# A decode step with cached attention: the pair loop rolled into seven rounds, batch by batch

## The chip, the cores and the metric

The kernel runs on one core of a Trainium2 chip. The time is device microseconds of one execution, the median over runs. The core has a matrix engine (PE, whose weight loads the profile lists apart as PEld), a vector engine (DVE), a scalar engine (ACT), a general engine (POOL) and SP, which here only issues loads. Sixteen DMA engines move the data from memory (HBM) into the on-chip store; each load that SP issues is spread over all of them.

## The reference

Eight batches, one new token each (x is 8 x 1 x 512). All arithmetic is in float32.

```python
xn = _layernorm(x)
# attention over a cache of 8192 positions, 8 KV heads of 128, 4 query heads on each
q = (xn @ wq).reshape(8, 1, 32, 128)
p = softmax(einsum("bhqd,bhkd->bhqk", q, repeat(k_cache, 4)) * 128 ** -0.5)
a = einsum("bhqk,bhkd->bhqd", p, repeat(v_cache, 4)).reshape(8, 1, 4096) @ wo
# token mixer on the same xn, hidden size 1792, inputs normalised once more
u = gelu(layernorm(xn)[..., None] * w1 + b1)      # (8, 512, 1792)
y = u @ w2 + b2
out = x + a + y
```

k_cache and v_cache are 8 x 8 x 8192 x 128 each, 268 MB apiece. Everything else is small beside them: wq and wo are 8.4 MB each.

## The kernel before, in words

**Pairs.** Two neighbouring KV heads of one batch form a pair: 8 MB of K and 8 MB of V. There are 32 pairs and one step for each (`duo_step`, L390). The order is by head group: pair i has group i // 8 and batch i % 8 (L105).

**Slots and loads.** The on-chip ring has five slots of 4 MB. K of a pair takes two slots, 1 and 2 or 0 and 1 in turn (`home`, L88); V takes slots 3 and 4. All loads of the caches are issued by SP in one queue, in an order written out by hand (`plan`, L93 to L101, taken by `load_next`, L103). A step n runs so:

1. First half of the scores (`score_half`, L381): for each quarter of the head dimension DVE transposes K in place in blocks of 32 (`turn_duo`, L255), and PE multiplies it with the query kept in `Z` (`qk_duo`, L261). After this half one slot is free, and SP issues the load of K for step n + 1.
2. Second half of the scores.
3. The row maximum (`top_duo`, L278), first half of the values of step n - 1 (`pv_duo`, L302: PE, with V as the moving operand), the exponential of step n on ACT (`exp_duo`, L283), second half of the values of step n - 1. Then slots 3 and 4 are free, and SP issues the load of V for step n.
4. `send_duo` (L296) lays the exponentials out for the next step's values: two PE matmuls, two DVE transposes.
5. At the end of a group of eight, `q_place_duo` (L242) fills `Z` for the next eight pairs. `place_duo` (L318) normalises and folds four finished pairs at a time into `OT`, which the output projection reads at the end. `take_duo` (L312) copies the finished values out of PE's accumulators.
6. `mix` (L365) does 5, 5 or 4 pieces of the token mixer: a gelu on ACT, and a scale and an addition on POOL (`mx_step`, L350). Fourteen pieces make a batch; `mx_begin` and `mx_end` are around them.

All engines run programs in the order written; the kernel is one straight line of instructions. PE's program is the longest: most matmuls in float32 are two passes, each with its weight load.

**Head and tail.** Before step 0 wq is loaded into slots 2 and 3, q is projected (`q_project`, L222), and 16 small matmuls on constants (`SHIFT`, L218 to L220) stand ahead of it. In the last step wo is loaded into free slots behind the last V, and the output projection follows as its pieces land.

The one function with all of this, with the line numbers of the profile:

## Time and profile before

| | |
|---|---|
| median of 3 runs | 1291.61 us (1291.28 to 1291.95) |
| profiled execution, its own time | 1291.54 us |
| its span, first to last instruction | 1289.5 us |
| granted clock of PE, mean | 0.803 |
| moved by DMA | 554.39 MB, 430 GB/s over the span |
| recorded instructions | 10806 |

The page gives, for each engine, busy time, share of the span and count of instructions; then the span in 40 slices; then the DMA queues. Queue q1 is SP's. Rows marked "instruction" are DMA packets that bring program code to the engines. In rows of instruction groups, the numbers after the first bar are busy time in us and the mean of one in ns, and after the second bar the engine's idle time before them with what ended it. "Landing" is the moment at which all of a load has arrived.

### The profile page before, as it was taken

The page shows a single profiled execution, that of the slowest core. Times are in us where ns is not written, and L with a number is a line of the kernel's source. Part 1 is how long each engine was busy: PE and PEld are TensorE (multiplying, and loading weights), DVE is VectorE, ACT ScalarE, POOL GpSimd, SP SyncE. Part 2 cuts the span into 40 slices and gives each one's busy share as a digit, 9 for nine tenths or more (in the row PEclk, how much of TensorE's full clock was granted, in tenths as well). Part 3 has the DMA queues.
Part 4 walks back from the last instruction along what each step waited for, and adds up shares of the span by engine and source line. Part 5 has one row for each costly group of instructions (what it writes and reads, how often), then busy time and mean ns, then how long its engine had stood idle before and what let it go on. Part 6 is the DMA issues. An engine that isn't in the chain of part 4 may idle for free.

```text
span 1289.5 us, 10806 instructions
## 1 busy us (share of the span) xinstructions
PE 755.4 (59%) x4662; PEld 161.9 (13%) x4662; DVE 677.8 (53%) x509; ACT 207.0 (16%) x311; POOL 226.5 (18%) x241
## 2 busy tenths in 40 slices
PE   4377455665456666565565656575454774466676
PEld 1111011111011111011110111111011110011112
DVE  3656654455644465654465644466644565544461
ACT  0002222121222121222111221212222000000000
POOL 0003323121332122233113322212332000000000
PEclk9667877997778896687886887877778878768879
DMA  9999999999999999999999999999999999999997
GB/s 407 433 431 448 427 427 438 434 431 438 431 431 440 431 427 444 425 432 442 427 434 438 431 434 434 436 436 427 436 434 431 432 436 435 429 440 432 427 428 323
DMA packets 11011, 554.39 MB, mean 430 GB/s; under 512 B 1324, under 2 KB 1356, under 8 KB 1748
## 3 DMA queue, kind: packets, MB, share of 16 engines
q1 hardware_dynamic: 10836, 553.67, 99.3%
q8 instruction: 36, 0.59, 0.2%
q14 instruction: 11, 0.09, 0.0%
q0 software_dynamic: 96, 0.02, 0.0%
q10 hardware_dynamic: 32, 0.02, 0.0%
HBM read 553.69 MB, written 0.02 MB: 429 GB/s over the span
## 4 chain that ended last, share of the span: by engine, by line
DMA 73%; DVE 22%; PE 4%; issue 0%; SPq 0%; DVEq 0%
DMA raw<-in_A_k_cache_dram 69%; DVE raw L257 22%; PE acc L267 3%; DMA raw<-in_A_wo_dram 2%; DMA raw<-in_A_wq_dram 2%; PE misc L227 0%; PE acc L308 0%; PE hb L444 0%; SPq L125 0%; DVEq L257 0%; SPq L82 0%; PE misc L285 0%; DVE macc L451 0%; DVEq L451 0%
## 5 line engine op out<-in xcount | busy, mean ns | idle before, releaser
L257 DVE STREAM_TRANSPOSE raw<-raw 128x2048 f32<-128x2048 f32 x256 | 565.4, 2275 | 242.0 <-DMA raw<-in_A_k_cache_dram 242.0
L267 PE MATMUL acc<-raw,z 128*32 128x512 f32 x2048 | 372.6, 812 | 481.4 <-DVE raw L257 480.1
L308 PE MATMUL acc<-raw,pt 128*32 128x512 f32 x2048 | 246.9, 624 | 12.0 <-DMA raw<-in_A_v_cache_dram 11.8
L354 POOL TENSOR_SCALAR g<-g,pad 128x512 f32<-128x512 f32 x112 | 77.8, 694 | 577.7 <-ACT g L353 577.7
L267 PEld LDWEIGHTS acc<-raw,z 128*32 128x32 f32 x2048 | 47.4, 124 | 789.9 <-DVE raw L257 491.2
L355 POOL TENSOR_TENSOR macc<-macc,g 128x512 f32<-128x512 f32 x112 | 142.0, 1268 | 9.3
L293 ACT ACTIVATE t2k<-acc,nb 128x512 f32<-128x512 f32 x32 | 22.0, 687 | 649.8 <-DVE nb L287 649.8
L300 DVE STREAM_TRANSPOSE pt<-misc 128x512 f32<-128x512 f32 x64 | 45.9, 717 | 141.3 <-PE misc L299 136.9
L353 ACT ACTIVATE g<-hb,pad 128x512 f32<-128x512 f32 x112 | 87.1, 777 | 192.8 <-POOL macc L355 191.5
L308 PEld LDWEIGHTS acc<-raw,pt 128*32 128x32 f32 x2048 | 66.2, 115 | 178.1 <-issue 150.0
L287 DVE CUSTOM_DVE_ANT_0 t2k<-misc,hmask 128x128 f32<-128x128 f32 x32 | 9.3, 291 | 122.5 <-PE misc L285 122.5
L299 PE MATMUL misc<-t2k,send 128*128 128x512 f32 x128 | 65.3, 633 | 2.7 <-ACT t2k L293 2.7
L280 DVE TENSOR_REDUCE mr<-acc 128x1 f32<-128x512 f32 x32 | 22.1, 690 | 50.8 <-PE acc L267 50.8
L316 ACT COPY ob<-acc 128x512 f32<-128x512 f32 x32 | 18.8, 586 | 118.9 <-PE misc L332 55.1
L347 POOL MEMSET macc<- 128x512 f32 x8 | 4.2, 527 | 182.0 <-PE misc L359 152.0
L353 ACT ACT_TABLE_LOAD x24 | 30.8, 1283 | 17.9 <-PE hb L345 17.6
L422 ACT ACT_TABLE_LOAD x24 | 30.8, 1283 | 0.4
L332 PE MATMUL misc<-ob,pick 128*32 128x512 f32 (+2 forms) x72 | 29.0, 545 | 0.7 <-ACT ob L316 0.7
L299 PEld LDWEIGHTS misc<-t2k,send 128*128 128x128 f32 x128 | 22.2, 193 | 44.7 <-issue 41.9
L334 DVE TENSOR_TENSOR t2k<-misc,keep 32x512 f32<-32x512 f32 (+2 forms) x9 | 5.7, 629 | 22.6 <-PE misc L332 22.6
L227 PE MATMUL misc<-raw,ob 128*32 128x512 f32 x64 | 10.4, 806 | 10.9 <-DMA raw<-in_A_wq_dram 10.9
L438 PE MATMUL acc<-raw,ot 128*32 128x512 f32 x56 | 8.0, 717 | 4.6 <-DMA raw<-in_A_wo_dram 4.6
(76 smaller groups left out, 122.4 us busy)
## 6 DMA issues: line engine op xcount, KB each, us to landing
raw<-in_A_v_cache_dram SPq DMA_DIRECT2D x4, 4096.0 KB, 35.5
raw<-in_A_wq_dram SPq DMA_DIRECT2D x2, 4096.0 KB, 17.2
raw<-in_A_k_cache_dram SPq DMA_DIRECT2D x2, 4096.0 KB, 31.9
raw<-in_A_wo_dram SPq DMA_DIRECT2D x1, 4096.0 KB, 28.6
raw<-in_A_wo_dram SPq DMA_DIRECT2D x1, 2048.0 KB
raw<-in_A_wo_dram SPq DMA_DIRECT2D x1, 1024.0 KB, 31.3
raw<-in_A_wo_dram SPq DMA_DIRECT2D x1, 512.0 KB
raw<-in_A_wo_dram SPq DMA_DIRECT2D x2, 256.0 KB, 32.3
```

The lines of the kernel that those rows point to most:

```text
L257: nc.vector.transpose(t, t)
L267: nc.tensor.matmul(SD[i][c * W:(c + 1) * W, :].rearrange("p (t j) -> p t j", j=W), Z[:, q, b, (1 - k) * REP:(1 - k) * REP + W], t[:, c * C ...
L280: nc.vector.tensor_reduce(mr, SD[i], AX.X, ALU.max)
L293: nc.scalar.activation(p, SD.pop(i), AF.Exp, bias=nb, scale=SCALE, accum_out=LD[e][:, o:o + 1])
L299: nc.tensor.matmul(m, send[:, k, :], p, start=True, stop=True)
L300: nc.vector.transpose(PT[k][:, :CH_T * W], m)
L308: nc.tensor.matmul(OD[i][j * W:(j + 1) * W, :].rearrange("p (c d) -> p c d", c=NCH), PT[k][:, t * W:(t + 1) * W], v[:, t], start=(not k an ...
L332: nc.tensor.matmul(mv, pick[:, c, :], ob[:, :n, c * DH:(c + 1) * DH], start=(c == 0), stop=(c == NCH - 1))
L353: nc.scalar.activation(g, hb, AF.Gelu_apprx_tanh, bias=b1t[:, j:j + 1], scale=w1t[:, j:j + 1])
L354: nc.gpsimd.tensor_scalar(g, g, w2t[:, j:j + 1], 1.0, op0=ALU.mult, op1=ALU.mult)
L355: nc.gpsimd.tensor_add(acc, acc, g)
L422: nc.scalar.activation(small.tile([P, 1], F32, name="warm"), nil, AF.Exp)
```

## The change

Pairs are taken batch by batch: pair i is batch i // 4 and head group i % 4, so that four steps in a row belong to one batch, and successive loads are successive 8 MB of the caches. Steps 0 and 1 and steps 30 and 31 stay written out. Steps 2 to 29 become a loop of seven rounds with four steps each. Inside it, the addresses of the loads, of the query taken for a batch, of the mixer's batch and of the output column come from registers. The loop is asked to synchronise its rounds by registers (`iteration_sync="reg_based"`).

- The query for all 32 pairs is put into `QZ` at the start, and `q_set` copies four pairs at a time into the smaller `Z`.
- The results of four pairs are normalised (`total`) and placed (`place_at`) together, once per batch, for one column of `OT`.
- The mixer does one batch per round, in pieces of 5, 5, 4 and 0; batch 7 is done ahead of the loop, seven pieces in each of the steps 0 and 1. The first piece writes `acc`, so that no clearing is needed; the scale is now a `tensor_tensor` with a broadcast operand.
- The bound of the exponential takes three DVE instructions in place of `tensor_tensor_reduce`.
- V of a round's fourth step, which the first step of the next round reads, is loaded on a semaphore `landed`. PE waits for it ahead of the values and takes the count back; before the loop PE raises it once for the first round. The other waits that the framework would make for this load are declared away (`apart`, `let_go`).
- The 16 matmuls on constants are gone.

```diff
+NG = HKV // 2
+FIRST = 2
+ROUNDS = B - 1
...
-MIX = (5, 5, 4)
+MIX = (5, 5, 4, 0)
...
-SHIFT = 16
...
+    pairs = {id(c): c.rearrange("b (g h) s d -> (b g) (h s d)", h=2) for c in (kc, vc)}
+    landed = tc.alloc_semaphore("landed")
+    def load(c, i, at, part=None, own=False):
+        flat = pairs[id(c)]
+        if isinstance(i, int):
+            rows = flat[i].rearrange("(p m) -> p m", p=P)
         else:
-            nc.sync.dma_start(t[:, x], rows[:, x])
+            rows = flat[bass.ds(i, 1)].rearrange("a (p m) -> p (a m)", p=P)
...
+        d = nc.sync.dma_start(slot(at, n).rearrange("p s m -> p (s m)"), rows)
+        if own:
+            d.then_inc(landed, 16)
+            tc.no_tile_sem_insts.add(d.ins.name)
+            tc.add_to_no_dep_group("landed", d.ins)
+        return d
...
-    idle = misc()
-    for j in range(SHIFT):
-        nc.tensor.matmul(idle[j % NB * W:(j % NB + 1) * W, :W], ident[:, :W], rep[:, 0, :W], start=True, stop=True)
...
+    def q_set(i, g, n):
+        dst = Z[:, :, :, REP:].rearrange("p g q (a k r) -> p g q a k r", k=2, r=REP)
         for a in range(NB):
             x = slice(a * W, (a + 1) * W)
-            nc.scalar.copy(dst[x, :, :, a, 0, :], src[x].rearrange("p (q b) r -> p q b r", b=B))
+            src = QZ[x, i:i + n] if isinstance(i, int) else QZ[x, bass.ds(i, n)]
+            nc.scalar.copy(dst[x, g:g + n, :, a, 0, :], src)
...
-        nc.vector.tensor_tensor_reduce(big()[:, :P], m[:, :P], hmask, -SCALE, 3.0e38, ALU.add, ALU.min, nb)
+        nc.vector.tensor_tensor(t, m[:, :P], hmask, op=ALU.add)
+        nc.vector.tensor_reduce(nb, t, AX.X, ALU.max)
+        nc.vector.tensor_scalar(ns, nb, -SCALE, None, op0=ALU.mult)
...
+    def total(lo, hi):
+        x = slice(lo * W, hi * W)
+        m = misc()
+        for g in range(lo, hi):
+            nc.tensor.matmul(m[g * W:(g + 1) * W, :1], ohg, lr[:, g:g + 1], start=True, stop=True)
+        nc.vector.reciprocal(rl[x], m[x, :1])
+    def place_at(lo, hi, col):
+        x = slice(lo * W, hi * W)
+        m = misc()
         for c in range(NCH):
+            for g in range(lo, hi):
+                nc.tensor.matmul(m[g * W:(g + 1) * W, :DH], pick[:, c, :], OB[:, g, c * DH:(c + 1) * DH],
+                                 start=(c == 0), stop=(c == NCH - 1))
...
     def mx_step(j):
         nc.scalar.activation(g, hb, AF.Gelu_apprx_tanh, bias=b1t[:, j:j + 1], scale=w1t[:, j:j + 1])
-        nc.gpsimd.tensor_scalar(g, g, w2t[:, j:j + 1], 1.0, op0=ALU.mult, op1=ALU.mult)
-        nc.gpsimd.tensor_add(acc, acc, g)
+        nc.gpsimd.tensor_tensor(g if j else acc, g, w2t[:, j:j + 1].to_broadcast([P, D]), op=ALU.mult)
+        if j:
+            nc.gpsimd.tensor_add(acc, acc, g)
...
+    def softmax_and_values(n, then, ready=None):
+        mr = top(n)
+        if ready is not None:
+            nc.tensor.wait_ge(landed, 16)
+            nc.tensor.sem_inc(landed, -16)
+        if n:
+            values(n - 1, 0, ready is not None)
+        p = exps(n, mr)
+        if n:
+            values(n - 1, 1, ready is not None)
+        d = then()
+        if ready is not None:
+            apart(d)
+        send_on(p)
...
-    for i in range(N_PR):
-        duo_step(i)
+    score_half(1, False)
+    softmax_and_values(1, lambda: load(vc, 1, 3))
+    nc.tensor.sem_inc(landed, 16)
+    take(0)
+    for j in range(NF // 2, NF):
+        mx_step(j)
+    warm()
+
+    with tc.For_i(FIRST, FIRST + ROUNDS * NG, NG, iteration_sync=SYNC) as i:
+        col = i - FIRST
+        j = 0
+        for n in range(FIRST, FIRST + NG):
+            score_half(n, True)
+            load(kc, i + (n + 1 - FIRST), home(n + 1))
+            score_half(n, False)
+            softmax_and_values(n, lambda: load(vc, i + (n - FIRST), 3, own=(n == FIRST + NG - 1)),
+                               n == FIRST or None)
+            take(n - 1)
+            if n == NG - 1:
+                total(0, NG)
+                q_set(i + (NG - FIRST), 0, NG)
+            if n == NG:
+                place_at(0, NG, col)
+            if n == FIRST:
+                mx_end(col * 2)
+                mx_begin(col)
+            for _ in range(MIX[n - FIRST]):
+                mx_step(j)
+                j += 1
+            warm()
```

## The prediction

> **What bounds the kernel now.** I read the page's busy lines and its DMA table first, then the chain of waits, then the last microseconds in windows, and then the timeline around one step boundary.

> The page:

> ```profile
> span 1289.5 us, 10806 instructions
> PE 755.4 (59%) x4662; PEld 161.9 (13%) x4662; DVE 677.8 (53%) x509; ACT 207.0 (16%) x311; POOL 226.5 (18%) x241
> GB/s 407 433 431 448 427 427 438 434 431 438 431 431 440 431 427 444 425 432 442 427 434 438 431 434 434 436 436 427 436 434 431 432 436 435 429 440 432 427 428 323
> q1 hardware_dynamic: 10836, 553.67, 99.3%
> q8 instruction: 36, 0.59, 0.2%
> q14 instruction: 11, 0.09, 0.0%
> ```

> No engine is over 59% busy, while the load queue q1 keeps all 16 DMA engines at 99.3% from the first slice to the last but one. So DMA sets the time, and a change in an engine's work counts only if a load is issued too late, or if DMA time itself changes. Two rows beside q1 are not data: 36 packets of 0.59 MB and 11 of 0.09 MB that fetch instructions. 0.59 MB is 63 bytes for each of PE's 4662 + 4662 instructions, so q8 is PE's code, one packet of 16.4 KB per 259 instructions, one about every 1289.5 / 36 = 35.8 us. q14 carries the other engines' code in packets of 8.2 KB.

> Does 0.2% of traffic matter? A load has landed only when the slowest of its DMA engines is done. The chain of waits (start us, length us, what) shows K loads from issue to landing:

> ```profile
> 266.22 28.58 DMA raw<-in_A_k_cache_dram
> ...
> 304.96 29.47 DMA raw<-in_A_k_cache_dram
> ...
> 615.46 29.69 DMA raw<-in_A_k_cache_dram
> ...
> 655.32 28.44 DMA raw<-in_A_k_cache_dram
> ...
> 887.29 29.53 DMA raw<-in_A_k_cache_dram
> ```

> Three of the five (those issued at 304.96, 615.46 and 887.29) take 0.9 to 1.2 us longer than the other two, 1.0 on the mean. They stand 310.5 and 271.8 us apart, which is 8.7 and 7.6 of PE's fetch intervals. I read that as PE's fetches going around eight DMA engines, with every eighth hitting the one that is already last. The windows over the end of the loads test it (columns: window, length, busy us of PE, PEld, DVE, ACT, POOL with counts, clock, DMA share, GB/s):

> ```profile
> 1278.00:1279.00 1.00, 1.00 (x8) 0.23 (x4) 0.00 (x0) 0.00 (x0) 0.00 (x0) 0.50 0.81 334
> 1279.00:1280.00 1.00, 1.00 (x12) 0.27 (x8) 0.00 (x0) 0.00 (x0) 0.00 (x0) 0.87 0.65 272
> 1280.00:1281.00 1.00, 1.00 (x12) 0.26 (x8) 0.00 (x0) 0.00 (x0) 0.00 (x0) 1.00 0.59 250
> 1281.00:1282.00 1.00, 1.00 (x16) 0.34 (x12) 0.00 (x0) 0.00 (x0) 0.00 (x0) 1.00 0.55 227
> 1282.00:1283.00 1.00, 0.97 (x12) 0.06 (x4) 0.00 (x0) 0.00 (x0) 0.00 (x0) 1.00 0.51 207
> 1283.00:1284.00 1.00, 0.76 (x8) 0.16 (x8) 0.00 (x0) 0.00 (x0) 0.00 (x0) 1.00 0.50 199
> 1284.00:1285.00 1.00, 0.84 (x20) 0.38 (x16) 0.00 (x0) 0.59 (x1) 0.00 (x0) 1.00 0.28 107
> 1285.00:1286.00 1.00, 0.96 (x28) 0.53 (x24) 0.00 (x0) 0.00 (x0) 0.00 (x0) 1.00 0.05 18
> ```

> A load's 128 equal rows give each of 16 engines the same share, yet the engines do not finish together: a fifth is done soon after 1278, half by 1283, and the last after 1285. The late half have run some 7 us behind the early ones. That spread is what the instruction packets have cost, as far as I can see: 36 / 8 = 4.5, so up to five hits on one engine, 7 / 5 = 1.4 us each. The other two readings of the price of a hit are 1.0 (the three long loads) and, from q8's share (0.15 to 0.25% of 16 x 1289.5 us over 36 packets), 0.86 to 1.43. I take 1.3, nearest to the end spread because that is the whole delay, and keep 0.86 and 1.43 as bounds.

> **The boundary between two steps.** This timeline (start, length, engine, line, idle before and its releaser) shows the cover that loop overhead would have:

> ```profile
> 633.16 1.98 PE L299 MATMUL misc<-t2k,send 128*128 128x512 f32 x4
> 633.29 0.33 SPq L111 DMA_DIRECT2D raw<-in_A_v_cache_dram  x1
> 634.32 1.57 DVE L300 STREAM_TRANSPOSE pt<-misc 128x512 f32<-128x512 f32 x2 [4.33 <-PE misc L299]
> 645.25 17.66 DVE L257 STREAM_TRANSPOSE raw<-raw 128x2048 f32<-128x2048 f32 x8 [9.35 <-DMA raw<-in_A_k_cache_dram]
> 647.82 3.72 PE L267 MATMUL acc<-raw,z 128*32 128x512 f32 x16 [12.08 <-DVE raw L257]
> 655.32 0.33 SPq L111 DMA_DIRECT2D raw<-in_A_k_cache_dram  x1
> 664.58 3.64 PE L308 MATMUL acc<-raw,pt 128*32 128x512 f32 x32 [0.56 <-DMA raw<-in_A_v_cache_dram]
> ```

> A K load is issued at 655.32 while the V load ahead of it lands near 664.5, when PE's wait for it ends, so the queue is about 9.2 us deep at that point. At the boundary DVE idles 9.35 us, PE 12.08, and SP issues nothing from 633.6 to 655.3. A late start of DVE costs DMA time only beyond 9.35 + 9.2 = 18.5 us.

> **The change part by part.** (1) *Code.* The unrolled steps 2 to 29 become one body run seven times. What PE executes per step, with the rows of ACT and POOL that part 5 needs:

> ```profile
> L267 PE MATMUL acc<-raw,z 128*32 128x512 f32 x2048 | 372.6, 812 | 481.4 <-DVE raw L257 480.1
> L308 PE MATMUL acc<-raw,pt 128*32 128x512 f32 x2048 | 246.9, 624 | 12.0 <-DMA raw<-in_A_v_cache_dram 11.8
> L299 PE MATMUL misc<-t2k,send 128*128 128x512 f32 x128 | 65.3, 633 | 2.7 <-ACT t2k L293 2.7
> L293 ACT ACTIVATE t2k<-acc,nb 128x512 f32<-128x512 f32 x32 | 22.0, 687 | 649.8 <-DVE nb L287 649.8
> L353 ACT ACTIVATE g<-hb,pad 128x512 f32<-128x512 f32 x112 | 87.1, 777 | 192.8 <-POOL macc L355 191.5
> L354 POOL TENSOR_SCALAR g<-g,pad 128x512 f32<-128x512 f32 x112 | 77.8, 694 | 577.7 <-ACT g L353 577.7
> L355 POOL TENSOR_TENSOR macc<-macc,g 128x512 f32<-128x512 f32 x112 | 142.0, 1268 | 9.3
> ```

> (2048 + 2048 + 128) / 32 + 1 = 133 matmuls, 266 instructions with weight loads, 1064 in four steps. The new per-batch work (placing four pairs, 16 calls of two passes; four sums; mixer begin and end) adds 88: about 1152, or 4.4 packets a round. If the body stays loaded from round to round, six of seven rounds fetch nothing: 36 - 6 x 4.4 = 9.6 packets are left, two at most on any of the eight engines instead of five. Three hits fewer at 1.3 us: **-3.9 us**, bounds 3 x 0.86 = -2.6 and 3 x 1.43 = -4.3. If it is fetched anew in each round, nothing is gained (rival 1). No row here shows a backward branch, so both stand; I take the first because the eight-way rotation of 16.4 KB packets looks like eight places of 256 instructions, and the body needs six at most.

> (2) *The loop itself*: branches, register additions, waits on registers, the first and last entry. No row shows them. From below: nothing, under the idle stretches above. From above: 18.5 us per round would have to be passed before any of it shows, so a few microseconds for refilling an engine's code are hidden too. What isn't hidden is setup before the first load (SP's first issue is on the path) and after the last. I take +0.2, 0 to 0.5. If the cover were gone, each us would cost 7.

> (3) *V on its own semaphore.* V of a round's fourth step is awaited by PE just ahead of the values matmuls, where the row at 664.58 waits for V already. Behind that wait stand those matmuls and, on SP, the next V load, as before. Cost 0; upper bound is rival 2.

> (4) *Order of pairs.* Each load is still 8 MB contiguous in 128 rows of 64 KB; only which one follows changes. 0, though a gain or loss inside HBM is not excluded: the load rate of 430 to 440 GB/s is flat over all head groups, so I allow 0.5 us either way.

> (5) *Mixer.* The multiplication becomes POOL TENSOR_TENSOR, 1268 instead of 694 ns by L355. A mix step is ACT's 777 ns and these two in turn, 0.78 + 0.69 + 1.27 = 2.74 us, and grows to 3.3, with the gaps between them some 3.5. Five steps take 2.9 us more, and ACT idles 649.8 / 32 = 20.3 us before each exponential: hidden. The first two steps now carry seven each, and there it is close:

> ```profile
> 75.49 3.78 PE L299 MATMUL misc<-t2k,send 128*128 128x512 f32 x4 [2.66 <-ACT t2k L293]
> 94.03 0.69 ACT L293 ACTIVATE t2k<-acc,nb 128x512 f32<-128x512 f32 x1 [18.50 <-DVE nb L287]
> 101.28 11.08 DVE L257 STREAM_TRANSPOSE raw<-raw 128x2048 f32<-128x2048 f32 x5 [1.44 <-DMA raw<-in_A_k_cache_dram]
> ```

> Step 0's send ends at 79.3 and the mixer's first matmuls a microsecond later; seven steps begun near 80.5 end near 102 to 105, so step 1's exponential comes about 10 us later than 94.03. PE's send and DVE's two small transposes stand behind it, and DVE would turn K(2) from about 108 instead of 101.28. That spends 6.6 of the 9.2 us of queue, once: +0.2, 0 to 1.

> (6) *Softmax bound.* One DVE instruction pair becomes three instructions. ACT's 20.3 us of idle time ahead of the exponential are spent waiting for DVE's result, so this one comes later by what the extra two cost. Bounds: nothing, and two short DVE instructions of the size of the 0.7 us transpose half above, 1.4 us; I take 0.5. Behind it stand the send and the small transposes, whose end at 635.9 has DVE's 9.35 us of idle time after it: hidden, as are the register-addressed copies of q on ACT, which has no mixer work in the fourth step. The dropped 16 idle matmuls only shorten the head.

> **Sum.** From the profiled execution's own 1291.54 (span 1289.5 and 2.0 around it; the median 1291.61 is the same to 0.1): -3.9 + 0.2 + 0.2 = -3.5, so **1288.0**. Its own range is 1286 to 1290.

> **Rivals.**
> 1. *The code is fetched again in every round* (the slower side). Place: q8 and q14. A round then fetches the five or six blocks it touches and perhaps one beyond: 42 to 49 packets in the loop and some 6 outside. Spread evenly that is 6 or 7 per DMA engine, +1.3 to +2.6 us; if a block always comes through the same engine, 8 or 9, +3.9 to +5.2. The small engines add to it: DVE's 64 compute instructions a round (by the code) with waits and registers span two packets of half the size, 14 to 21 in all, and through one engine at 0.65 us that is 9 to 14 us, up to 7 over today's spread. It decides from the sixth hit on one engine. Time 1293 to 1299, middle 1295. For: nothing in the trace shows code being kept. Against: the rotation over eight. [...]
> 2. *Something still waits for V at the round's edge.* PE would start its scores with V at 664.6 instead of 647.8, the four quarters take 4 us, and the K load goes out near 669, 4.5 us after the queue ran dry: with some 1.9 us to restart (what the first slice lost: 407 of 433 GB/s over 32.2 us) 6.4 us a round, 1288.0 + 45 = 1333; at the first entry alone, 1294.4. Against: the change gives V its own semaphore.
> 3. *Fetches don't set the pace* (the late finish of half the engines has another cause). Then the sum is +0.4: 1292. Against: the spacing of the long loads.

> **Chances.** Forecast 0.56, rival 1 0.25, rival 2 0.08, rival 3 0.11. About 0.2% (2.6 us) is what a measurement tells from no change: below 1289.0 is faster, above 1294.2 slower. Faster: most of the forecast's share, 0.50. Slower: two thirds of rival 1 and most of rival 2, 0.24. Within: 0.26. For 8 in 10 the range runs from 1285.5 (one hit left per engine) to 1297 (most of rival 1).

> **What would show it.** q8 near 10 packets with q14 below 11; no K load longer than its neighbours by 1 us; DMA share falling to nothing within some 3 us at the end instead of 7. Rival 1: q8 at 45 or more and a spread over 7 us. Rival 2: a hole in DMA's share once a round. I am wrong if q8 falls to 10 and the time stays.

## The result, and the profile after

The changed kernel takes 1300.57 us (1299.37 to 1301.66) against 1291.57: a ratio of 1.0068, 95% interval 1.0055 to 1.0081, so 9 us slower. The forecast was 1288.0, with a range from 1285.5 to 1297; the measured time lies above it, on the other side of the kernel before.

The page after, the rows that answer to those of before:

```profile
span 1298.1 us, 12560 instructions
GB/s 405 436 436 277 419 423 443 424 436 436 426 446 426 444 424 444 426 426 446 426 446 424 444 424 438 434 426 446 426 444 424 444 426 426 446 426 447 423 427 354
q1 hardware_dynamic: 10836, 553.67, 98.6%
q8 instruction: 11, 0.18, 0.0%
q14 instruction: 3, 0.02, 0.0%
```

The data are the same 553.67 MB. PE's code, q8 (it rose from 36 packets to 52 in the run below that adds 4096 PE instructions), came in 11 packets where there were 36, and q14 shows 3 where there were 11. But one slice, the fourth, moved 277 GB/s. Windows over it (columns as in the prediction; the last two are DMA share and GB/s):

```profile
110.00:115.00 5.00, 0.00 (x0) 0.00 (x0) 5.00 (x3) 0.78 (x1) 3.95 (x4) 0.61 1.00 433
115.00:120.00 5.00, 0.00 (x0) 0.00 (x0) 5.00 (x3) 1.55 (x2) 3.14 (x4) 0.50 0.58 249
120.00:125.00 5.00, 0.00 (x0) 0.00 (x0) 5.00 (x4) 0.78 (x1) 3.95 (x4) 0.50 0.00 0
125.00:130.00 5.00, 4.47 (x32) 1.42 (x36) 1.66 (x1) 2.26 (x3) 2.69 (x3) 0.68 0.01 2
130.00:135.00 5.00, 5.00 (x53) 1.51 (x45) 0.69 (x1) 0.00 (x0) 0.00 (x0) 1.00 0.82 301
135.00:140.00 5.00, 5.00 (x49) 1.48 (x45) 0.73 (x3) 0.78 (x2) 0.00 (x0) 1.00 1.09 472
```

DMA lost 5 x (0.42 + 1.00 + 0.99 + 0.18 - 0.09) = 12.5 us, once. In the kernel before, the same stretch is full:

```profile
115.00:120.00 5.00, 2.75 (x24) 0.36 (x16) 3.94 (x2) 0.00 (x0) 0.00 (x0) 0.87 0.97 419
120.00:125.00 5.00, 5.00 (x41) 1.08 (x33) 0.69 (x1) 0.00 (x0) 0.00 (x0) 0.79 1.03 446
```

In the changed kernel PE did nothing for the first 15 of these 30 us, while DVE went on turning K. The timeline there:

```profile
94.88 0.33 SPq L116 DMA_DIRECT2D raw<-in_A_v_cache_dram  x1
...
103.22 0.67 ACT L304 ACTIVATE t2k<-acc,ns 128x512 f32<-128x512 f32 x1
...
105.77 0.78 ACT L360 ACTIVATE g<-hb,pad 128x512 f32<-128x512 f32 x1
...
109.00 17.66 DVE L275 STREAM_TRANSPOSE raw<-raw 128x2048 f32<-128x2048 f32 x8 [0.42 <-issue]
...
125.41 0.78 ACT L360 ACTIVATE g<-hb,pad 128x512 f32<-128x512 f32 x1 [2.50 <-POOL macc L363]
125.53 8.36 PE L284 MATMUL acc<-raw,z 128*32 128x512 f32 x64 [17.71 <-ACTq L425]
...
130.82 0.35 SPq L116 DMA_DIRECT2D raw<-in_A_k_cache_dram  x1
```

L425 is the loop's own line. At the first entry PE's first scores stood 17.7 us behind something that ACT's sequencer does at L425, and that came 0.1 us after ACT had started the last of its seven gelu pieces of step 1 (105.77 to 125.41). It is not POOL that was awaited: its part of that piece ended only at 128.7. The K load behind these scores was issued at 130.82, where the kernel before issued it at 112.17. No other slice of the loop is under 419 GB/s, and from 140 to 1180 us the rate is 434 GB/s, as before (the changed kernel first, then the kernel before):

```profile
140.00:1180.00 1040.00, 589.62 (x3858) 123.80 (x3854) 565.27 (x424) 177.03 (x274) 217.33 (x189) 0.80 1.00 434
140.00:1180.00 1040.00, 612.77 (x3735) 126.92 (x3736) 561.06 (x384) 182.70 (x268) 207.71 (x215) 0.81 1.00 434
```

### The profile page after: what moved, and what is told of

Same layout as the page of the kernel before. It is cut to its first block, busy times and chain, and to the rows that moved or that the text cites. A ratio compares the mean times of both kernels' runs of the same rounds, so it can differ in the third digit from the quotient of the medians.

```text
span 1298.1 us, 12560 instructions
## 1 busy us (share of the span) xinstructions
PE 732.7 (56%) x4860; PEld 163.8 (13%) x4860; DVE 681.9 (53%) x557; ACT 208.0 (16%) x328; POOL 250.9 (19%) x225
## 3 DMA queue, kind: packets, MB, share of 16 engines
q1 hardware_dynamic: 10836, 553.67, 98.6%
## 5 line engine op out<-in xcount | busy, mean ns | idle before, releaser
L284 PE MATMUL acc<-raw,z 128*32 128x512 f32 x2048 | 367.4, 803 | 490.0 <-DVE raw L275 383.4
L322 PE MATMUL acc<-raw,pt 128*32 128x512 f32 x2048 | 240.1, 610 | 16.7 <-DMA raw<-in_A_v_cache_dram 12.9
L361 POOL TENSOR_TENSOR g<-g,pad 128x512 f32<-128x512 f32 x104 | 108.1, 1039 | 375.7 <-ACT g L360 375.7
L363 POOL TENSOR_TENSOR macc<-macc,g 128x512 f32<-128x512 f32 x104 | 132.0, 1269 | 8.2
L304 ACT ACTIVATE t2k<-acc,ns 128x512 f32<-128x512 f32 x32 | 22.0, 687 | 673.4 <-PE acc L322 603.4
L360 ACT ACTIVATE g<-hb,pad 128x512 f32<-128x512 f32 x112 | 87.1, 778 | 216.1 <-POOL macc L363 202.3
L361 POOL TENSOR_TENSOR macc<-g,pad 128x512 f32<-128x512 f32 x8 | 8.3, 1039 | 526.6 <-ACT g L360 526.6
L298 DVE TENSOR_TENSOR t2k<-misc,hmask 128x128 f32<-128x128 f32 x32 | 9.3, 292 | 113.8 <-PE misc L296 113.8
L360 ACT ACT_TABLE_LOAD x23 | 29.5, 1283 | 38.8 <-PE hb L356 38.6
L373 ACT ACT_TABLE_LOAD x23 | 29.5, 1283 | 0.4
L356 PE MATMUL hb<-hn,hsel 8*128 8x512 f32 x16 | 9.9, 702 | 7.3 <-DVE hsel L355 7.3
L369 PE MATMUL misc<-macc,esel 128*8 128x512 f32 x16 | 8.1, 590 | 8.1 <-DVE esel L367 8.1
L346 DVE TENSOR_TENSOR t2k<-misc,keep 128x128 f32<-128x128 f32 (+2 forms) x9 | 2.6, 292 | 18.3 <-PE misc L343 18.3
## 6 DMA issues: line engine op xcount, KB each, us to landing
raw<-in_A_wo_dram SPq DMA_DIRECT2D x1, 1024.0 KB, 32.2
```

The lines of the kernel that those rows point to most:

```text
L284: nc.tensor.matmul(SD[n][c * W:(c + 1) * W, :].rearrange("p (t j) -> p t j", j=W), Z[:, n % NG, q, (1 - k) * REP:(1 - k) * REP + W], t[:, ...
L304: nc.scalar.activation(p, SD.pop(n), AF.Exp, bias=ns, scale=SCALE, accum_out=lr[:, n % NG:n % NG + 1])
L322: d = nc.tensor.matmul(OD[n][j * W:(j + 1) * W, :].rearrange("p (c d) -> p c d", c=NCH), PT[k][:, t * W:(t + 1) * W], v[:, t], start=(not ...
L360: nc.scalar.activation(g, hb, AF.Gelu_apprx_tanh, bias=b1t[:, j:j + 1], scale=w1t[:, j:j + 1])
L361: nc.gpsimd.tensor_tensor(g if j else acc, g, w2t[:, j:j + 1].to_broadcast([P, D]), op=ALU.mult)
L363: nc.gpsimd.tensor_add(acc, acc, g)
```

## The experiments

**The mixer's pieces away from the entry.** Theory A: PE's wait at the entry is for ACT to enter the loop, which it does only after its last pieces. Rival B: it is for V, or for the loop's setup.

```diff
+    EARLY = (4, 10)
+    mx_begin((B - 1) * BS)
+    for j in range(EARLY[0]):
+        mx_step(j)
     for q in range(NB):
         turn(0, 0, q)
     q_project()
...
     q_set(0, 0, NG)
+    for j in range(*EARLY):
+        mx_step(j)
+    warm()
...
     softmax_and_values(0, lambda: None)
-    mx_begin((B - 1) * BS)
-    for j in range(NF // 2):
+    for j in range(EARLY[1], NF):
         mx_step(j)
...
     take(0)
-    for j in range(NF // 2, NF):
-        mx_step(j)
     warm()
```

> The 14 mixer pieces of batch 7 are moved off the loop's entry: four ahead of the projection of q, six after the first copy of q, four after step 0, none in step 1. Theory A (PE's first scores in the loop wait until ACT has entered the loop, which it does only after its last seven pieces; the hole of 12.5 us in DMA's share near 118 to 132 is this wait): the hole goes, 1300.6 - 12.5 = 1288.0, between 1287 and 1289; PE's wait of 14 us at the entry falls under 1 us. Rival B (what is awaited at the entry is the V load of step 1, or the loop's setup itself): PE starts its scores no earlier than V's landing, a hole of 6 us or more stays, 1294 to 1301.

Measured: 1287.29 us, ratio 0.9964 (0.9951 to 0.9977) to the kernel before: faster than both kernels. Its timeline at the entry, and the windows that held the hole:

```profile
96.51 0.59 ACT L329 COPY ob<-acc 128x512 f32<-128x512 f32 x1 [1.91 <-PE acc L322]
...
101.49 17.66 DVE L275 STREAM_TRANSPOSE raw<-raw 128x2048 f32<-128x2048 f32 x8 [2.37 <-DMA raw<-in_A_k_cache_dram]
104.01 3.94 PE L284 MATMUL acc<-raw,z 128*32 128x512 f32 x16 [5.65 <-issue]
...
111.88 0.35 SPq L116 DMA_DIRECT2D raw<-in_A_k_cache_dram  x1
```

```profile
115.00:120.00 5.00, 4.09 (x24) 0.38 (x20) 4.15 (x2) 0.00 (x0) 0.00 (x0) 0.70 0.97 419
120.00:125.00 5.00, 4.25 (x41) 1.42 (x41) 0.69 (x1) 0.00 (x0) 0.00 (x0) 1.00 0.97 419
```

PE follows DVE's first turn, the K load goes out at 111.88, and the hole is gone. Rival B falls in both its forms. V of step 1 stands in the queue behind the K whose landing let DVE start at 101.49, and its 8 MB take some 19 us more at the 434 GB/s measured, so PE did not wait for it. And the loop's setup costs nothing here: PE starts 2.5 us behind DVE, as in the kernel before (645.25 and 647.82).

**Half of it: the seven pieces of step 1 left out.** The other seven stay after step 0. The kernel leaves these seven out altogether, so its result lacks them.

```diff
     take(0)
-    for j in range(NF // 2, NF):
-        mx_step(j)
     warm()
```

> The changed kernel without the seven mixer pieces of step 1; those seven of batch 7 are left out of the sum. Theory A: ACT enters the loop at about 104.5 us; the first seven pieces still make step 1's exponential late, so that DVE turns K(2) from 109 instead of 101.3 and the next K load goes out near 119, a microsecond after the queue has run dry: a hole of about 3 us, 1291. Rival B: the hole stays at 12.5 us, 1300.

Measured: 1288.68 us, 0.9975 (0.9965 to 0.9985). The K load is issued at 119.82, as expected, and a hole remains, shorter than expected:

```profile
115.00:120.00 5.00, 3.32 (x24) 0.36 (x16) 5.00 (x3) 0.00 (x0) 0.00 (x0) 0.82 0.61 262
120.00:125.00 5.00, 2.18 (x20) 0.36 (x23) 5.00 (x4) 0.00 (x0) 0.00 (x0) 1.00 1.08 419
```

That is 5 x (0.39 - 0.08) = 1.6 us, and the time is 1.4 above the kernel with the mixer early. So of the entry's 13.3 us (1300.57 - 1287.29) the late exponential of step 1 has cost 1.4, and ACT's late entry 11.9.

**The rounds written out.** Everything else as in the changed kernel, the mixer's sevens too; no load uses `landed`.

```diff
-    with tc.For_i(FIRST, FIRST + ROUNDS * NG, NG, iteration_sync=SYNC) as i:
+    for i in range(FIRST, FIRST + ROUNDS * NG, NG):
```

> The changed kernel with the seven rounds written out one after the other, constant addresses and ordinary waits, everything else as in it. Theory A: no entry to a loop, so ACT's lateness costs only what step 1's late exponential costs (about 3 us), and PE's code is fetched in some 37 packets again: 1291.6 + 3 = 1294.5, between 1292 and 1296. Rival C (the batch-by-batch order or the other edits cost the time, not the loop): 1300 or more.

Measured: 1293.92 us, 1.0014 (1.0004 to 1.0023), with q8 at 38 packets. The order of pairs and the other edits don't cost 9 us; the loop does, and by the two runs above it is its entry.

**Code alone.** To the kernel before, small matmuls on constants are added where PE idles.

```diff
+MORE = 32
...
         send_duo(p)
+        more = misc()
+        for j in range(MORE):
+            nc.tensor.matmul(more[j % NB * W:(j % NB + 1) * W, :W], ident[:, :W], rep[:, 0, :W], start=True, stop=True)
```

> The kernel before with 32 more small matmuls on constants a step, on PE between the send and the next scores, where PE idles 12 us: 128 more PE instructions a step, 4096 in all, 16 more code packets, and no other use of DMA. Theory D (a code packet delays the DMA engine it comes through by 1.3 us, and the slowest of eight sets the time): two more hits on each, 1291.6 + 2.7 = 1294.3, between 1293.3 and 1294.8. Rival (fetches don't set the pace): 1291.6.

Measured: 1294.43 us against 1291.69, 1.0021 (1.0013 to 1.0030): 2.7 us for sixteen packets. Two on each of eight DMA engines, at the 1.3 us that the prediction took, give 2.6.

```profile
q8 instruction: 52, 0.85, 0.2%
```

**V on an ordinary wait.** From here on the kernel with the mixer early (1287.29) is the base. The wait and the counts on `landed` go too.

```diff
-            softmax_and_values(n, lambda: load(vc, i + (n - FIRST), 3, own=(n == FIRST + NG - 1)),
-                               n == FIRST or None)
+            softmax_and_values(n, lambda: load(vc, i + (n - FIRST), 3, own=False))
```

> The kernel with the mixer moved early (1287.3), and V of a round's fourth step on an ordinary wait, not on a semaphore of its own. If ordinary waits across the round's edge are taken ahead of the first instruction of the next round, PE starts its scores with V's landing, some 19 us after K's, and each of six edges costs 6.4 us of DMA (rival 2 of the prediction): 1287.3 + 38 = 1325, between 1315 and 1335. If they are taken at the values matmuls, nothing changes: 1287.3.

Measured: 1300.76 us, 1.0067 (1.0050 to 1.0084). Neither expectation came true: the six inner edges cost nothing, and one hole stands at the loop's exit.

```profile
1195.00:1200.00 5.00, 0.00 (x0) 0.00 (x0) 0.00 (x0) 0.00 (x0) 0.00 (x0) 0.50 1.00 433
1200.00:1205.00 5.00, 0.00 (x0) 0.00 (x0) 1.48 (x1) 0.00 (x0) 0.00 (x0) 0.50 0.06 26
1205.00:1210.00 5.00, 3.85 (x16) 0.43 (x16) 5.00 (x3) 0.00 (x0) 0.00 (x0) 0.50 0.01 3
```

All five engines stand idle until the last V has landed, and the queue is empty. The trace records for each load when each DMA engine has finished its share; for this V the last record is at 1202.8. DVE starts to turn the next K 0.7 us later, so that the K load behind it goes out at 1213.59:

```profile
1203.52 17.66 DVE L270 STREAM_TRANSPOSE raw<-raw 128x2048 f32<-128x2048 f32 x8 [29.13 <-PEq L512]
...
1213.59 0.35 SPq L111 DMA_DIRECT2D raw<-in_A_k_cache_dram  x1
```

So here the loop's exit waited for a load that was started in it: DVE's 29.13 us of idle time ended 0.7 us after that load's last record. The semaphore of its own takes V out of that: it is worth 1300.76 - 1287.29 = 13.5 us, once.

**Eight pieces at each edge.**

```diff
-MIX = (5, 5, 4, 0)
+MIX = (2, 2, 2, 8)
```

> The kernel with the mixer moved early, and the pieces of a round spread 2, 2, 2, 8 instead of 5, 5, 4, 0, so that ACT comes to each round's edge only after eight pieces, some 26 us after its copy of the values. Theory A1 (only the first entry needs ACT's arrival; inside the loop PE waits for single instructions of ACT): no change, 1286.8 to 1288. Theory A2 (PE waits at each round's start until ACT has come around): the K load of each round goes out some 13 us late, 4 to 6 us of hole at six edges, 1312 to 1323.

Measured: 1298.49 us, 1.0049 (1.0032 to 1.0065). A2 falls: no hole at the inner edges. But the time is outside A1's range too, which had not counted the exit. The exit here waits for ACT's and POOL's eighth piece of the last round:

```profile
1196.42 0.78 ACT L360 ACTIVATE g<-hb,pad 128x512 f32<-128x512 f32 x1 [2.49 <-POOL macc L363]
...
1198.39 1.26 POOL L363 TENSOR_TENSOR macc<-macc,g 128x512 f32<-128x512 f32 x1
...
1200.52 17.66 DVE L275 STREAM_TRANSPOSE raw<-raw 128x2048 f32<-128x2048 f32 x8 [26.39 <-PEq L519]
```

DVE starts 0.9 us after POOL's last addition has ended, and 2 us before V's last record (1202.6), so it is not V that is awaited. The windows:

```profile
1200.00:1205.00 5.00, 1.93 (x8) 0.23 (x8) 4.48 (x3) 0.00 (x0) 0.00 (x0) 0.50 0.00 0
1205.00:1210.00 5.00, 4.39 (x20) 0.61 (x24) 5.00 (x4) 0.00 (x0) 0.00 (x0) 0.50 0.01 3
```

The changed kernel has 0 in the fourth place of MIX, and no such hole at its exit.

**How much code stays loaded.** Two runs lengthen the loop's body by small matmuls on constants, 32 a step (the diff) and 64 a step. The 2048 in the two expectations is 8 x 256, the prediction's estimate from the rotation over eight and some 256 instructions a packet (259 by its count); no run had shown it yet.

```diff
             softmax_and_values(n, lambda: load(vc, i + (n - FIRST), 3, own=(n == FIRST + NG - 1)),
                                n == FIRST or None)
+            more = misc()
+            for x in range(32):
+                nc.tensor.matmul(more[x % NB * W:(x % NB + 1) * W, :W], ident[:, :W], rep[:, 0, :W], start=True, stop=True)
             take(n - 1)
```

> The kernel with the mixer moved early, and 32 small matmuls on constants more in each of the four steps of the loop: 512 more PE instructions in the body, about 1700 in all, under 2048. If eight blocks of 256 instructions stay loaded, the body is fetched once: two code packets more than the 11 there are, 1287.3 to 1288.7. If fewer stay, each round fetches 7 to 8: q8 near 55 and 1293 to 1297.

> As before it with 64 small matmuls a step: 1024 more PE instructions, about 2200 in the body, over 2048. If eight blocks of 256 stay loaded, a round of nine to ten blocks finds little or nothing left of it: q8 at 60 to 75, eight to nine hits on each of eight DMA engines instead of two, at 1.35 us each 1295 to 1298. If more stay, 1287.3 to 1289 with q8 at 15.

Measured: 1287.19 us (0.9963, 0.9949 to 0.9977) with some 1700 PE instructions in the body, and 1298.12 us (1.0047, 1.0030 to 1.0063) with some 2200. The pages of the two, first the shorter body:

```profile
q8 instruction: 13, 0.21, 0.1%
```

```profile
q8 instruction: 70, 1.15, 0.3%
```

Two packets more for 512 instructions that run seven times: the body was fetched once. With 1024 more, some nine packets come in every round, which is the whole body (2200 / 259 = 8.5), so nothing of it is left when it starts anew; and the time rises by 10.8 us. PE's work in itself does not explain that: the 64 matmuls are (816.3 - 738.0) / 28 = 2.8 us of PE's busy time a step, in a gap of 9 to 12 us, and half as many cost nothing.

What a packet does is seen in the records of the single DMA engines, 16 for each load. In the kernel before, the last engine finishes its share behind the first by 1.8 us when 8 packets of q8 have come, by 3.2 after 16, 4.6 after 24 and 6.0 after 32, and it jumps by 1.0 us right after each of these, at the 9th, 17th, 25th and 33rd packet; eight packets add (6.0 - 1.8) / 3 = 1.4 us. In the run with 2200 instructions, after 32 packets, eight engines are 0 to 1.5 us behind the first and the other eight 5.8 to 6.0. From there on the spread levels off at 6 to 7.6 us and the first engines fall behind as well (by 6 us near 1207), so it no longer counts the packets. With the mixer early, no packet comes from 204 to 1191 us, and the spread stays at 1.7 to 1.8; in the changed kernel none comes from 218 to 1205 us, and it stays at 1.8 to 1.9 from 270 to 1197. So PE's packets went around eight engines here, and each delayed its engine by some 1.4 us.

**The rounds written out, with the mixer early.** This differs from the 1287.29 us kernel by the loop alone, and with it by the semaphore: V is on ordinary waits, which above cost nothing but at the loop's exit, and here there is none.

```diff
-    with tc.For_i(FIRST, FIRST + ROUNDS * NG, NG, iteration_sync=SYNC) as i:
+    for i in range(FIRST, FIRST + ROUNDS * NG, NG):
```

> The kernel with the mixer moved early (1287.3), and the seven rounds written out with ordinary waits; it differs from it by the loop alone. Theory A and D: no hole anywhere, and the code packets come back (11 to about 38, five hits in place of two on the slowest DMA engine): 1287.3 + 3 x 1.35 = 1291.4, between 1290.5 and 1292. If part of the 4 us came from the order of pairs, the smaller query copy or the mixer's new place, it stays below 1290.5.

Measured: 1291.58 us, 0.9996 (0.9987 to 1.0005) of the kernel before, with q8 at 38 packets. The order of pairs, the query copy, the three DVE instructions and the longer mixer pieces cost and gain nothing together; the loop's code gains 1291.58 - 1287.29 = 4.3 us.

## Why the prediction was wrong, point by point

**(1) Code: right.** q8 fell to 11 (forecast near 10), the body stayed loaded, and the loop's code gave -4.3 us, at the upper bound of 2.6 to 4.3 and near the -3.9 taken. The price of a hit holds against added packets too (2.7 us for 16), and the records of the single engines give 1.4 us, within its bounds of 0.86 and 1.43. The sign that the prediction named is there: at the end of the changed kernel's loads DMA's share falls to nothing in some 3 us instead of 7.

```profile
1291.00:1292.00 1.00, 0.81 (x12) 0.16 (x8) 0.00 (x0) 0.00 (x0) 0.00 (x0) 1.00 1.00 399
1292.00:1293.00 1.00, 0.86 (x8) 0.00 (x0) 0.00 (x0) 0.07 (x1) 0.00 (x0) 1.00 0.62 240
1293.00:1294.00 1.00, 0.97 (x32) 0.75 (x32) 0.00 (x0) 0.52 (x1) 0.00 (x0) 1.00 0.33 127
1294.00:1295.00 1.00, 0.64 (x16) 0.16 (x8) 0.17 (x1) 0.00 (x0) 0.00 (x0) 1.00 0.00 0
```

Rival 1, code fetched anew in every round, is what happened with the longest body, as the run with some 2200 instructions shows (70 packets). Its time of 1298.12 lies in that rival's range of 1293 to 1299, but by another sum: the rival got its upper end from the small engines, whose q14 shows 4 packets there, and q8 has 70 instead of 48 to 55. Rival 3 falls by the same runs. The shorter bodies, some five and seven blocks of 256 instructions long, brought 11 and 13 packets. The prediction's eight places of 256 were its estimate; the runs agree with it, and show that the limit lies between some 1700 and some 2200 instructions, no more closely.

**(2) The loop itself: this step failed.** It priced the first entry and all else that shows at 0.2 us, 0 to 0.5, by the idle stretches of a middle step. At the entry PE's first scores stood 17.7 us until ACT passed the loop's first line, and ACT's program has seven pieces, 20 us, ahead of that line. The idle time of DVE and PE at a step's boundary (9.35 and 12.08 us) is the cover for work of their own; it was no cover for the wait on ACT, whose queue was still full. So the 18.5 us of cover, DVE's idle time and the depth of the queue in one sum, did not hold for this wait: DVE was already at work, and PE started 16.5 us behind it instead of 2.5. Of the queue's 9.2 us, step 1's late exponential had left nothing: in the run without the second seven the K load went out at 119.82 and DMA had already run dry. It went out 11.0 us later here. The step asked what each engine would have to execute at the edge and not whom it would wait for there. What it cost: 11.9 us.

**(5) The mixer: right mechanism, wrong place for its end.** Step 1's exponential came at 103.22 (forecast 102 to 105) and DVE turned K(2) from 109.00 (forecast about 108). Alone this cost 1.4 us, for which the term was 0.2, 0 to 1. Written out, the same lateness cost 1293.92 - 1291.58 = 2.3 us, with single runs from 1292.58 to 1294.58; so the split of the entry's 13.3 us into 1.4 and 11.9 is good to about 1 us. The other seven pieces, behind step 1, got no price of their own in the prediction; what they delayed was the loop's entry.

**(3) and rival 2.** V at the six inner edges costs nothing, with the semaphore or without it; its use is at the exit, 13.5 us, which the prediction did not see. Rival 2 allowed for the shape of what happened, a hole at the first entry alone, but blamed V and priced it at 6.4 us (1294.4).

**(4) and (6): right**, as far as their sum goes, by the rounds written out with the mixer early, at 1291.58; the two were not taken apart.

Sum of what was measured: 1291.6 - 4.3 + 1.4 + 11.9 = 1300.6. It closes by itself, as each term is the difference of two neighbouring runs; the terms stand on the traces.

The exact dependence behind ACT's arrival, whether `Z`, an accumulator, `lr` or the loop's own bookkeeping, was not separated; the runs show that ACT's queue ahead of the entry sets it.

## What to carry to other kernels

Where DMA is busy throughout, as here (q1 at 98.6 to 99.3%), program code is traffic too: count its packets by DMA engine. Here one more packet on the slowest of them cost the whole kernel some 1.3 to 1.4 us, and a loop of up to some 1700 PE instructions took most of them away (36 packets before, 11 and 13 with a loop). Before a loop is entered or left, look at every engine's queue, not at the one that needs the next result: work that is off the path in straight code can be on it at such a line, as ACT's mixer pieces were at the entry (11.9 us), and V's load (13.5 us) and the last pieces (1298.49 - 1287.29 = 11.2 us) at the exit. Moving filler work ahead of that line by some tens of microseconds turned 9 us lost into 4.3 us gained.

## What the runs showed of the hardware that was not expected

```profile
L361 POOL TENSOR_TENSOR g<-g,pad 128x512 f32<-128x512 f32 x104 | 108.1, 1039 | 375.7 <-ACT g L360 375.7
L363 POOL TENSOR_TENSOR macc<-macc,g 128x512 f32<-128x512 f32 x104 | 132.0, 1269 | 8.2
```
